# First block of a fused Fourier mixing and MLP kernel: the last product of each weight rounding on GpSimd, the other operations of the rounding reordered

## The chip, the cores and the metric

The kernel runs on one core of one Trainium2 chip. The metric is the device time in microseconds (us) of one execution; the median of three runs counts. The five engines of a core (TensorE, VectorE, ScalarE, GpSimd, SyncE; in the profile PE, DVE, ACT, POOL, SP) each work through an own queue in order and wait for each other by semaphores.

## The reference

```python
def reference(x, moe_w_in, moe_w_out):          # x: 8 x 3008 x 256, f32
    X = np.fft.fft(x, axis=1)
    X = np.fft.fft(X, axis=2)
    a = X.real.astype(np.float32).reshape(8 * 3008, 256)
    h = a @ moe_w_in                             # 256 x 2048
    g = np.maximum(h, 0.0) ** 2
    return (g @ moe_w_out).astype(np.float32)    # 2048 x 256
```

The two weight matrices arrive as 64-bit floats. The kernel reads each as pairs of 32-bit words (`low`, `high`) and rounds them to f32 on the chip.

## The kernel before, in words

The Fourier transform along the sequence is a set of matrix products with tables of cosines and sines. Symmetries are folded first, so that for each of the 8 sequences only 1505 columns remain; they lie in two tiles `Pt` and `Qt`, and a third, `Et`, holds one column spread over all partitions. The transform along the 256 features is merged into the first weight matrix: G1 and G2 are the products of the cosine and sine tables with `moe_w_in`.

After an opening (tables, the fold and transform of the first sequence, up to about 43 us) the kernel runs one long list of steps. A step is (sequence, block of 251 columns, j), with j from 0 to 7 (`NJ`), each j standing for two chunks of 128 of the 2048 hidden features. One step has these parts:

- `front`: for both chunks, TensorE multiplies `Pt` by G1 and `Qt` by G2 into a PSUM tile `ph` (L825, L826; two such tiles take turns). VectorE adds the `Et` part (L828, tile `he`) and forms sum and difference (L830, L831, tile `g`).
- `combine`: ScalarE takes relu and square of `g` (L840, L841). From step 8 on GpSimd also forms four sums `s` (L848 to L851) for a scheme with seven instead of eight products.
- `back`, two steps later (`LAG = 2`): TensorE multiplies `g` by `wout` into accumulators (L865 in the first block, with eight products a step; L878 with seven afterwards).

The first block (steps 0 to 7, sequence 0, columns 0 to 250) has more to do, since the weights are prepared there, just in time. For each j one tile `win` and one tile `wout` of 128 x 512 are loaded (`load`, SyncE, L259, into tiles `raw`) and rounded (`convert`). A rounding of one tile has, in the kernel before, eight operations on 128 x 512 elements: VectorE takes the exponent out of `high` (L274, tile `fd`); ScalarE turns it into a scale by two relus (L276, L277); VectorE takes the mantissa bits (L279, tile `m`); ScalarE scales `low` in place (L281); and then the function `finish` on VectorE puts the sign in (L284), adds `low` to the mantissa (L286) and multiplies mantissa and scale into the target (L287). Tiles `fd` come from a pool of two, tiles `m` from a pool of three.

`begin_win(j)` starts the rounding of `win` j; its second function `products` (TensorE L302, ScalarE L303) makes the chunks of G1 and G2, and its third, `for_e` (TensorE L311, VectorE L313), the factor `gE` that L828 uses. `load_wout(j)` starts the rounding of `wout` j.

The order within each engine's queue is the order of the Python calls; no scheduler changes it. In a step i of the first block `weights` calls, after `front`: the products of `win` i+1; the start of `wout` i-1; the end of `win` i+2 (`rounded`); the start of `win` i+3. The end of `wout` i-1 comes last in the step (`leftover`), ahead of L313 of `win` i+1. So VectorE has this order in a step: front, start of `wout`, end of `win`, start of the next `win`, end of `wout`, L313.

From step 10 on, VectorE and ScalarE fold the next sequence between the fronts (`ahead`, `between`).

Of the kernel before, what the change touches and what calls it, by code (L numbers as in the profile page):

```python
# [8 lines left out]
F32 = mybir.dt.float32  # L9
U32 = mybir.dt.uint32  # L10
AF = mybir.ActivationFunctionType
ALU = mybir.AluOpType
# [70 lines left out]
def kernel(  # L83
# [12 lines left out]
    nc = tc.nc  # L96
    B, NROW, _, D = x.shape
# [6 lines left out]
    NJ = NFC // 2  # L104
# [19 lines left out]
    op = ctx.enter_context(tc.tile_pool(name="op", bufs=2))  # L124
# [5 lines left out]
    tt = nc.vector.tensor_tensor  # L130
    act = nc.scalar.activation
# [81 lines left out]
    for i in range(2):  # L213
        nc.vector.tensor_scalar(out=signs[:, i:i + 1], in0=last, scalar1=(-2.0, 2.0)[i], scalar2=(1.0, -1.0)[i],
                                op0=ALU.mult, op1=ALU.add)
# [15 lines left out]
    def pair_in(j):  # L231

        return moe_w_in.rearrange("(c p) (h j f) -> j c p h f", p=P, j=NJ, h=2)[j]
# [5 lines left out]
    def parts(w, k):  # L239
        return w.rearrange("p c (e h) -> p h (c e)", h=k)  # L240
# [6 lines left out]
    def scratch():  # L247

        return sp.tile([P, 4 * CK], F32, name="m", tag="s")[:, 0:2 * CH].rearrange("p (c e) -> p c e", c=2)

    def load(src):

        nonlocal raws
        pool, tag = (gp, "g") if raws in (1, 2) else (xp, "x") if raws % (NX + 1) else (ep, "c")
        raws += 1
        single = src.dtype == F32
        raw = pool.tile([P, 2, CH, 1 if single else 2], src.dtype if single else U32, name="raw", tag=tag)
        for c in range(2):
            nc.sync.dma_start(out=raw[:, c].rearrange("p (o e) w -> p o (e w)", o=src.shape[2]),  # L259
                              in_=src[c] if single else src[c].bitcast(U32))  # L260
        return raw

    def convert(dst, raw):


        k = dst.shape[1]
        if raw.dtype == F32:
            return lambda: nc.vector.tensor_copy(dst, parts(raw[:, :, :, 0], k))
        low, high = raw[:, :, :, 0], raw[:, :, :, 1]
        m = scratch()  # L270
        e = fp.tile([P, 2, CH], F32, name="fd", tag="fd")
        mb, eb, rest = m.bitcast(U32), e.bitcast(U32), low.bitcast(F32)

        nc.vector.tensor_scalar(out=eb, in0=high, scalar1=20, scalar2=0x7FF,  # L274
                                op0=ALU.logical_shift_right, op1=ALU.bitwise_and)
        act(e, eb, AF.Relu, bias=ramp[:, 0:1], scale=-1.0)  # L276
        act(eb, e, AF.Relu, bias=ramp[:, 1:2], scale=-2.0 ** 23)  # L277

        nc.vector.tensor_scalar(out=mb, in0=high, scalar1=0xFFFFF, scalar2=0x100000,  # L279
                                op0=ALU.bitwise_and, op1=ALU.bitwise_or)  # L280
        act(rest, low, AF.Copy, scale=2.0 ** -32)  # L281

        def finish():
            nc.vector.scalar_tensor_tensor(out=eb, in0=high, scalar=0x80000000, in1=eb,  # L284
                                           op0=ALU.bitwise_and, op1=ALU.bitwise_or)
            tt(out=m, in0=mb, in1=rest, op=ALU.add)  # L286
            nc.vector.scalar_tensor_tensor(out=dst, in0=parts(m, k), scalar=2.0 ** -20, in1=parts(e, k),  # L287
                                           op0=ALU.mult, op1=ALU.mult)

        return finish  # L290


    def begin_win(j):

        w = ep.tile([P, 2, CH], F32, name="win", tag="sB" if j % 2 else "sA")
        finish = convert(parts(w, 1), win.pop(j, None) or load(pair_in(j)))

        def products():
            for tab, G, nm in ((cosd, G1, "mC"), (sind, G2, "mD")):
                pg = psm.tile([P, CH], F32, name="pg", tag=nm)  # L300
                for i in range(2):
                    nc.tensor.matmul(pg, tab[:, i], w[:, i], start=i == 0, stop=i == 1)  # L302
                nc.scalar.copy(G.rearrange("p (h j f) -> j p h f", h=2, j=NJ)[j],  # L303
                               pg.rearrange("p (h f) -> p h f", h=2))

        def for_e():

            ps = psd.tile([P, CH], F32, name="pe", tag="d")
            for h in range(2):
                fc = j + NJ * h  # L310
                nc.tensor.matmul(ps[:, h:h + 1], G2[:, fc * P:(fc + 1) * P], last, start=True, stop=True)  # L311

            return lambda: nc.vector.tensor_scalar_mul(gE[:, j::NJ], ps[:, 0:2], 0.5)  # L313

        win[j] = finish, products, for_e

    win = {}

    def load_wout(j):

        return convert(wout[:, j].rearrange("p h c e -> p h (c e)"), load(pair_out(j)))
# [477 lines left out]
    def spread_e():  # L799

        _, qt, et = PQE[0]
        ps = psd.tile([P, CH], F32, name="pe", tag="d")[:, 0:CK]
        nc.tensor.matmul(ps, last.to_broadcast([P, P]), qt[:, 0:CK], start=True, stop=True)
        nc.scalar.copy(et[:, 0:CK], ps)
# [10 lines left out]
    def front(b, k0, n, j, between):  # L815

        pt, qt, et = PQE[b]
        ks = slice(k0, k0 + n)
        g = gp.tile([P, 2, 2, CK], F32, name="g", tag="g")
        for h in range(2):  # L820
            fc = j + NJ * h
            fs = slice(fc * P, (fc + 1) * P)
            ps = psh.tile([P, 2, CH], F32, name="ph", tag="h")
            hP, hQ = ps[:, 0, 0:n], ps[:, 1, 0:n]
            nc.tensor.matmul(hP, G1[:, fs], pt[:, ks], start=True, stop=True)  # L825
            nc.tensor.matmul(hQ, G2[0:P - 1, fs], qt[0:P - 1, ks], start=True, stop=True)  # L826
            t = hp.tile([P, CK], F32, name="he", tag="he")[:, 0:n]
            nc.vector.scalar_tensor_tensor(out=t, in0=et[:, ks], scalar=gE[:, fc:fc + 1], in1=hP,  # L828
                                           op0=ALU.mult, op1=ALU.add)
            tt(out=g[:, h, 0, 0:n], in0=t, in1=hQ, op=ALU.add)  # L830
            tt(out=g[:, h, 1, 0:n][:, ::-1], in0=t, in1=hQ, op=ALU.subtract)  # L831
            between(h)
        return g
# [179 lines left out]
                groups[1, kp, nm]()  # L1013

    def rounded(j):
        win[j][0]()


    start()
# [50 lines left out]
    q_part("even0", "even1", "even2")  # L1070
    awake(12)
    rounded(1)
    for kp in range(2):
        for nm in ("join_4", "join_2", "lo"):
            groups[1, kp, nm]()
        if kp == 0:
            begin_win(2)
    spread_e()
    q_part("hi")
    copy_e()  # L1080
# [10 lines left out]
    def share(i):  # L1091
        return 0.0 if i < NJ + LAG + 2 else SHARE[i % NJ]
# [17 lines left out]
            f()  # L1110
            spent, room = spent + t, room - t

    late = []

    def weights():


        if i + 1 < NJ:
            win[i + 1][1]()
        now = i - 1 if i < NJ - 1 else i  # L1120
        if now >= 0:
            late.append(load_wout(now))
        if i + 2 < NJ:
            rounded(i + 2)
        if i + 3 < NJ:
            begin_win(i + 3)
        elif i == NJ - 2:
            late.append(load_wout(i))

    def leftover():  # L1130
        while late:
            late.pop(0)()

    flight, finished = [], []
    for i in range(len(steps) + LAG + 4):
        if i < len(steps):
            b, k0, n, j = steps[i]
            if i == NJ:
                for k in range(NX):
                    load_later(k)  # L1140
            if NJ <= i < NJ + NL:
                load_column(i - NJ)
            if i % per == 0:
                assert not side
                side = ahead(b + 1) if b + 1 < B else []
                spent, pace = 0.0, sum(t for t, _ in side) / sum(share(i + k) for k in range(per - 2))
            g = front(b, k0, n, j, between)
            if i < NJ:
                weights()
                s = combine(n, g, True)  # L1150
            elif i < 2 * NJ:
                leftover()
                if j < 4:
                    sum_wout(slice(j // 2 * (NJ // 2), (j // 2 + 1) * (NJ // 2)), j % 2)
        while finished and finished[0][0] <= i:
            store(*finished.pop(0)[1:])
        if i >= LAG and flight:
            at, g_, s_ = flight.pop(0)
            final = at[:3] == (B - 1, *BLOCKS[-1])
            back(at[2], at[3], g_, s_, final)  # L1160
            if at[3] == NJ - 1:
                c_ = gather(at[2], s_ is None, final)
                finished += [(i + 2 + s, *at[:3], s, c_, final) for s in range(2)]
        if i + 1 < NJ:
            late.append(win[i + 1][2]())
            leftover()
        if i < len(steps):
            flight.append(((b, k0, n, j), g, s if i < NJ else combine(n, g, False)))
# [63 lines left out]
```

## Time and profile before

| | before |
|---|---|
| median of 3 runs | 1924.22 us (1923.99 to 1924.96) |
| the profiled execution | 1924.01 us, of which span 1922.2 us |
| TensorE busy | 1909.9 us, 99% of the span |
| VectorE busy | 1451.7 us, 76% |
| ScalarE busy | 957.3 us, 50% |
| GpSimd busy | 1110.5 us, 58% |
| mean granted TensorE clock | 0.999 |
| L287, 128 x 512, first block | 16 times, 0.69 to 0.70 us each |
| L284 and L286 | 16 times each, 0.69 us each |
| L274 and L279 | 16 times each, 0.42 us each |

The span runs from the first to the last instruction; the execution's time has 1.8 us around it. The busy time of an instruction is longer than its place in the queue where the next one may start before it ends: four L274 or L279 in a row start 0.335 us apart, two independent operations of 0.69 us start 0.60 us apart. A wait in the profile names the instruction that waited, the one that released it, and the time that its engine stood idle.

### The profile page before, as it was taken

How to read it: one execution, taken by the hardware profiler on the slowest of the kernel's cores; microseconds unless marked ns; L12 is line 12 of the kernel's file. 1: busy time of each engine (PE TensorE's matmuls, PEld its weight loads, DVE VectorE, ACT ScalarE, POOL GpSimd, SP SyncE). 2: the span in 40 equal slices, each digit the busy share in tenths (PEclk: the TensorE clock that was granted, in tenths of full speed). 3: DMA queues.
4: the chain of work that ended last, by engine and by line, in shares of the span. 5: the costliest groups of instructions: out<-in, count | busy, mean ns of one | idle time of the engine just before them, and what ended most of it. 6: DMA issues, size and time to landing. Idle time of an engine off the chain costs nothing.

```text
span 1922.2 us, 28182 instructions
## 1 busy us (share of the span) xinstructions
PE 1909.9 (99%) x9270; PEld 1700.5 (88%) x9270; DVE 1451.7 (76%) x3654; ACT 957.3 (50%) x1209; POOL 1110.5 (58%) x1701
## 2 busy tenths in 40 slices
PE   9999999999999999999999999999999999999998
PEld 7888898888988898888988889888898888988887
DVE  8998887887677876788668887788767877655554
ACT  2855554455454554545445454455544555444444
POOL 0055665666566655665665666566656666566565
PEclk9999999999999999999999999999999999999999
DMA  8331111110111101111011110111001101100100
GB/s 216 117 38 37 44 40 31 34 41 17 28 36 35 40 12 36 28 47 28 12 36 39 39 26 12 45 37 36 21 20 46 36 12 22 27 12 12 22 11 23
DMA packets 146622, 69.58 MB, mean 36 GB/s; under 512 B 130145, under 2 KB 137259, under 8 KB 146474
## 3 DMA queue, kind: packets, MB, share of 16 engines
q1 hardware_dynamic: 146022, 66.87, 14.0%
q8 instruction: 73, 1.20, 0.3%
q14 instruction: 75, 0.61, 0.1%
q0 software_dynamic: 176, 0.65, 0.1%
q10 hardware_dynamic: 276, 0.26, 0.0%
HBM read 43.03 MB, written 24.69 MB: 35 GB/s over the span
## 4 chain that ended last, share of the span: by engine, by line
PE 94%; DVE 3%; DMA 1%; issue 0%; ACT 0%; SPq 0%; DVEq 0%; ACTq 0%
PE ph L825 16%; PE ph L826 16%; PE mC L878 16%; PE mA L878 16%; PE mB L878 16%; PE mD L878 8%; PE pd L727 1%; PE pd L619 1%; PE pd L701 1%; DMA xt<-in_x_dram 1%; DMA cosT<-in_cos_s_dram 0%; DVE he L828 0%; DVE m L286 0%; DVE g L831 0%; DMA sind<-in_sin_d_dram 0%
## 5 line engine op out<-in xcount | busy, mean ns | idle before, releaser
L840 ACT ACTIVATE g<-g 128x1004 f32<-128x1004 f32 (+1 forms) x384 | 399.0, 1039 | 689.4 <-DVE g L831 425.2
L848 POOL TENSOR_TENSOR s<-g 128x251 f32<-128x251 f32 (+1 forms) x376 | 237.2, 631 | 689.8 <-ACT g L841 628.3
L828 DVE SCALAR_TENSOR_TENSOR he<-Et,gE,ph 128x251 f32<-128x251 f32 (+1 forms) x768 | 362.4, 472 | 340.4 <-PE ph L826 336.0
L825 PE MATMUL ph<-Pt,G 128*128 128x251 f32 (+1 forms) x1536 | 453.2, 376 | 0.0
L826 PE MATMUL ph<-Qt,G 127*128 127x251 f32 (+1 forms) x1536 | 452.2, 375 | 0.0
L841 ACT ACTIVATE g<-g 128x1004 f32<-128x1004 f32 (+1 forms) x384 | 399.3, 1040 | 12.2
L878 PE MATMUL mC<-s,wsum 128*128 128x251 f32 (+1 forms) x1504 | 381.4, 374 | 0.0
L878 PE MATMUL mA<-g,wout 128*128 128x251 f32 (+1 forms) x1504 | 380.1, 374 | 0.0
L830 DVE TENSOR_TENSOR g<-he,ph 128x251 f32<-128x251 f32 (+1 forms) x768 | 320.3, 417 | 53.5 <-DVE he L828 1.8
L826 PEld LDWEIGHTS ph<-Qt,G 127*128 127x128 f32 x1536 | 291.9, 190 | 35.9
L825 PEld LDWEIGHTS ph<-Pt,G 128*128 128x128 f32 x1536 | 285.8, 189 | 34.3 <-DVE g L831 0.4
L878 PEld LDWEIGHTS mC<-s,wsum 128*128 128x128 f32 x1504 | 285.5, 190 | 34.5
L831 DVE TENSOR_TENSOR g<-he,ph 128x251 f32<-128x251 f32 (+1 forms) x768 | 314.0, 409 | 0.0
L878 PEld LDWEIGHTS mA<-g,wout 128*128 128x128 f32 x1504 | 282.6, 189 | 35.3 <-issue 0.3
L849 POOL TENSOR_TENSOR s<-s,g 128x251 f32<-128x251 f32 (+1 forms) x376 | 271.5, 722 | 29.5
L850 POOL TENSOR_TENSOR s<-g 128x251 f32<-128x251 f32 (+1 forms) x376 | 273.2, 726 | 0.0
L851 POOL TENSOR_TENSOR s<-g,s 128x251 f32<-128x251 f32 (+1 forms) x376 | 241.6, 643 | 0.0
L878 PE MATMUL mB<-g,wsum 128*128 128x251 f32 (+1 forms) x752 | 220.5, 374 | 0.0
L878 PE MATMUL mD<-s,wout 128*128 128x251 f32 (+1 forms) x752 | 220.3, 374 | 0.0
L878 PE MATMUL mB<-s,wout 128*128 128x251 f32 (+1 forms) x752 | 219.9, 374 | 0.0
L878 PEld LDWEIGHTS mB<-g,wsum 128*128 128x128 f32 x752 | 142.6, 190 | 17.4
L878 PEld LDWEIGHTS mD<-s,wout 128*128 128x128 f32 x752 | 141.9, 189 | 17.7
(174 smaller groups left out, 1389.0 us busy)
## 6 DMA issues: line engine op xcount, KB each, us to landing
out_dram<-os SPq DMA_DIRECT2D x376, 56.0 KB
xt<-in_x_dram SPq DMA_DIRECT2D x39, 384.0 KB
xt<-in_x_dram SPq DMA_DIRECT2D x63, 128.0 KB
Et<-e_dram SPq DMA_DIRECT2D x7, 752.5 KB
out_dram<-os SPq DMA_DIRECT2D x288, 6.8 KB
raw<-in_moe_w_in_dram SPq DMA_DIRECT2D x16, 256.0 KB
raw<-in_moe_w_out_dram SPq DMA_DIRECT2D x16, 256.0 KB
xt<-in_x_dram SPq DMA_DIRECT2D x2, 512.0 KB
```

The costliest lines, as they stand in the source:

```text
L825: nc.tensor.matmul(hP, G1[:, fs], pt[:, ks], start=True, stop=True)
L826: nc.tensor.matmul(hQ, G2[0:P - 1, fs], qt[0:P - 1, ks], start=True, stop=True)
L828: nc.vector.scalar_tensor_tensor(out=t, in0=et[:, ks], scalar=gE[:, fc:fc + 1], in1=hP, op0=ALU.mult, op1=ALU.add)
L830: tt(out=g[:, h, 0, 0:n], in0=t, in1=hQ, op=ALU.add)
L831: tt(out=g[:, h, 1, 0:n][:, ::-1], in0=t, in1=hQ, op=ALU.subtract)
L840: act(v, v, AF.Relu)
L841: act(v, v, AF.Square)
L848: gt(out=s1, in0=g21, in1=g22, op=ALU.add)
L849: gt(out=s2, in0=s1, in1=g11, op=ALU.subtract)
L850: gt(out=s3, in0=g11, in1=g21, op=ALU.subtract)
L851: gt(out=s4, in0=g12, in1=s2, op=ALU.subtract)
L878: nc.tensor.matmul(acc[nm][:, i, 0:n], w, v[:, 0:n], start=j == 0 and i == 0, stop=j == NJ - 1, skip_group_check=True)
```

## The change

The rounding changes in three ways. First, its arithmetic: ScalarE now scales the mantissa in place (L281: `m` by 2^-20) instead of `low`; the addition becomes one operation that scales `low` by 2^-52 and adds `m`; the last product becomes a plain product of two tiles, which any engine with a product can do. `convert` returns two functions, `halves` (sign and addition, VectorE) and `product(engine)`.

Second, the engine: in the first block the product is done by GpSimd; the two roundings of the opening (`win` 0 and 1) keep it on VectorE.

Third, the order. What was started in step i-1 is ended at the beginning of step i, ahead of its front (`rounding`): the `halves` of the tile started last come first, the products come in the order of the starts. After the front, `weights` calls the products of `win` i+1, the start of `win` i+3 and the start of `wout` i (step 5 starts `wout` 5 and 6, step 6 `wout` 7). So VectorE has this order in a step: `halves` of `wout` i-1, `halves` of `win` i+2, front, start of `win` i+3, start of `wout` i, L313. In the changed kernel the line numbers behind the rounding are one higher (L825 becomes L826, L311 becomes L312).

```diff
@@ convert
-        mb, eb, rest = m.bitcast(U32), e.bitcast(U32), low.bitcast(F32)
+        mb, eb = m.bitcast(U32), e.bitcast(U32)
...
-        act(rest, low, AF.Copy, scale=2.0 ** -32)
-
-        def finish():
+        act(m, mb, AF.Copy, scale=2.0 ** -20)
+
+        def halves():
             nc.vector.scalar_tensor_tensor(out=eb, in0=high, scalar=0x80000000, in1=eb,
                                            op0=ALU.bitwise_and, op1=ALU.bitwise_or)
-            tt(out=m, in0=mb, in1=rest, op=ALU.add)
-            nc.vector.scalar_tensor_tensor(out=dst, in0=parts(m, k), scalar=2.0 ** -20, in1=parts(e, k),
-                                           op0=ALU.mult, op1=ALU.mult)
-
-        return finish
+            nc.vector.scalar_tensor_tensor(out=m, in0=low, scalar=2.0 ** -52, in1=m, op0=ALU.mult, op1=ALU.add)
+
+        def product(engine):
+            engine.tensor_tensor(out=dst, in0=parts(m, k), in1=parts(e, k), op=ALU.mult)
+
+        return halves, product
@@ rounded (opening)
-        win[j][0]()
+        halves, product = win[j][0]
+        halves()
+        product(nc.vector)
@@ the steps
-    late = []
+    late, open_ = [], [begun]          # begun: win 2, started in the opening
+
+    def rounding():
+
+        for halves, _ in reversed(open_):
+            halves()
+        while open_:
+            open_.pop(0)[1](nc.gpsimd)
 
     def weights():
         if i + 1 < NJ:
             win[i + 1][1]()
-        now = i - 1 if i < NJ - 1 else i
-        if now >= 0:
-            late.append(load_wout(now))
-        if i + 2 < NJ:
-            rounded(i + 2)
         if i + 3 < NJ:
             begin_win(i + 3)
-        elif i == NJ - 2:
-            late.append(load_wout(i))
+            open_.append(win[i + 3][0])
+        for k in (i, i + 1)[i > NJ - 3:1 + (NJ - 3 <= i < NJ - 1)]:
+            open_.append(load_wout(k))
...
+            if i < NJ:
+                rounding()
             g = front(b, k0, n, j, between)
             if i < NJ:
                 weights()
                 s = combine(n, g, True)
             elif i < 2 * NJ:
-                leftover()
```

## Prediction before the run

> **What bounds the kernel now.** I read the page first: its chain that ended last gives the split of the whole span.
>
> ```profile
> PE 94%; DVE 3%; DMA 1%; issue 0%; ACT 0%; SPq 0%; DVEq 0%; ACTq 0%
> ```
>
> TensorE carries nearly everything. The change touches only the first block (steps 0 to 7, about 43 to 98 us). So the second view is busy time by stretch, cut to that block: PE, PEld, DVE, ACT, POOL, then the granted clock.
>
> ```profile
> 46.70:53.00 6.30, 4.14 (x20) 3.40 (x20) 6.09 (x16) 4.42 (x9) 0.00 (x0) 1.00 0.28 102
> 53.00:57.00 4.00, 3.85 (x13) 3.25 (x14) 3.78 (x9) 3.93 (x8) 0.00 (x0) 0.61 0.42 131
> 64.40:71.60 7.20, 7.20 (x37) 6.46 (x36) 6.95 (x17) 5.81 (x10) 0.00 (x0) 1.00 0.34 113
> 71.60:78.90 7.30, 7.30 (x38) 6.51 (x38) 7.01 (x17) 5.94 (x10) 0.00 (x0) 1.00 0.40 136
> 86.20:94.00 7.80, 7.47 (x37) 6.33 (x36) 7.01 (x17) 5.23 (x10) 0.00 (x0) 1.00 0.18 67
> ```
>
> TensorE is full from 57 to 86 us and has holes only before and after. The third view, the waits, prices them.
>
> ```profile
> PE pe L311 <- ACT G L303: 2.7, 2, 2.3
> PE mA L865 <- DVE wout L287: 0.6, 1, 0.6
> ```
>
> So TensorE loses 3.3 us to waits. The granted clock fell after the 2.3 us hole: (1 - 0.61) x 4.00 = 1.56 us lost there, and 0.15 more in the next stretch (0.98 over 7.4 us), 1.7 in all. 5.0 us is therefore about all that a faster VectorE could win here. The fourth view is VectorE's queue over one step, in order of time.
>
> ```profile
> 72.79 0.48 DVE L828 SCALAR_TENSOR_TENSOR he<-Et,gE,ph 128x251 f32<-128x251 f32 x1
> ...
> 75.12 0.42 DVE L274 TENSOR_SCALAR fd<-raw 128x512 uint32<-128x512 uint32 x1
> ...
> 76.40 0.69 DVE L286 TENSOR_TENSOR m<-m,raw 128x512 f32<-128x512 uint32 x1
> 77.12 0.69 DVE L287 SCALAR_TENSOR_TENSOR win<-m,fd 128x512 f32<-128x512 f32 x1
> ...
> 79.84 0.69 DVE L287 SCALAR_TENSOR_TENSOR wout<-m,fd 128x512 f32<-128x512 f32 x1
> 80.72 0.47 DVE L828 SCALAR_TENSOR_TENSOR he<-Et,gE,ph 128x251 f32<-128x251 f32 x1
> ```
>
> One step of VectorE is 80.72 - 72.79 = 7.93 us with no idle gap; TensorE needs 7.27 us (L302's first start goes 64.36, 71.63, 78.90). VectorE drifts later by 0.66 us a step while TensorE works off its lead. What matters of the old order: between a rounding's first operations (L274, L279) and its last ones VectorE always has another weight tile's operations, so ScalarE's three operations in between are hidden.
>
> **What the change removes.** Per step the two products (L287) leave VectorE: each spans 0.72 us from start to next start, 1.4 us in all. The remaining work of a step is front 75.12 - 72.79 = 2.33, four starts at 0.335, four `halves` operations at 0.60, one L313 at 0.2: 6.3 us, below TensorE's 7.27. L286 becomes another two-input operation of the same shape (0.68 against 0.69 for the neighbouring forms), and ScalarE's L281 now reads and writes `m` at the same 512 elements: an operation of the same size on the same engine replaces each, so both cost nothing. The same holds for the two roundings of the opening, whose product stays on VectorE.
>
> **What it moves.** In the new order VectorE's queue in a step is: front(i), L274 and L279 of `win` i+3, L274 and L279 of `wout` i, L313, then the `halves` of that `wout`, then of that `win`, then front(i+1). Between the starts and the first `halves` only L313 is left. The `halves` of `wout` need ScalarE's six operations (three for `win`, then three for `wout`), and in VectorE's queue the next front is behind them. That is a walk from VectorE to ScalarE and back inside each step. The loads move no queue: SyncE still issues `win` 3, `wout` 0, `win` 4, `wout` 1 and so on, each when a raw tile comes free, which now happens after the `halves`, a step ahead of the use; before, the last ones were issued by 85.4 us. The last `wout` roundings leave step 8 for steps 6 and 7, so the x tiles of the next sequence, which reuse those buffers and are first read in step 10, do not come later relative to the steps. ScalarE does two roundings back to back in one place of the trace:
>
> ```profile
> 52.99 0.73 ACT L276 ACTIVATE fd<-fd,ramp 128x512 f32<-128x512 uint32 x1
> ...
> 56.32 0.66 ACT L281 ACTIVATE raw<-raw 128x512 f32<-128x512 uint32 x1
> ```
>
> That is 56.32 + 0.66 - 52.99 = 3.99 us. The walk, from one L274 to the next step's L274: L274 to ScalarE's L276 0.46 (75.12 to 75.58), six operations 3.99, signal 0.04, then L286 of `wout`, L284 and L286 of `win` 3 x 0.60 = 1.80, front 2.33: **8.62 us a step** against 7.93 before and TensorE's 7.27. Behind the waiting `halves` stand the front's L828, so the ph buffers come free late and TensorE waits for them.
>
> From the start: L313 at 43.07, two `halves` of `win` 2 (ScalarE finished it at 42.02) to 44.42, so front 0 starts at 44.42 (43.81 before), and L274 of `win` 3 at 46.75. Front 1 is 4.49 + 1.80 = 6.29 later, at 53.04 (48.99 before). Front 6 is 5 x 8.62 later, 96.14 (87.89 before). Step 6 rounds one tile only: front 2.33, then 0.46 + 0.76 + 0.62 + 0.68 + 0.04 = 2.56, L286 0.60, front 7 at 101.63. TensorE's front 8 needs the first ph buffer of front 7, 0.85 + 0.41 + 0.04 = 1.30 later: 102.93, where before it started at 97.76. With 0.14 more between the halves of that front (a wait of 0.32 against 0.18 before) the sum is **+5.3 us**. From there TensorE is full in both, so nothing is won back. The 3.3 us of waits and the 1.7 us of slow clock are inside the old 97.76 and are not added again; a slow stretch early in the block would be hidden, as TensorE waits 1.3 us a step anyway.
>
> **What it adds.** Two products a step on GpSimd. No row has that shape. Nearest:
>
> ```profile
> L850 POOL TENSOR_TENSOR s<-g 128x251 f32<-128x251 f32 (+1 forms) x376 | 273.2, 726 | 0.0
> 46.08 0.57 POOL L809 DMA_DIRECT2D Et<-e_dram  x1 [1.94 <-DMA e_dram<-Qt]
> ```
>
> 251 elements take 0.63 (L848) to 0.72. Scaled by 2.04 that is 1.47 at most; with 0.10 fixed, as the smallest memset (103 ns), 0.63 gives 0.53 x 2.04 + 0.10 = 1.18. GpSimd is otherwise empty in this block, after the two `e_dram` transfers it issues until 46.65. `win` i+2 is needed a step later and `wout` i two fronts later, so the product's length alone is hidden behind the walk. It is not hidden from VectorE:
>
> ```profile
> 153.56 0.64 POOL L851 TENSOR_TENSOR s<-g,s 128x251 f32<-128x251 f32 x1
> 153.80 0.67 DVE L492 TENSOR_TENSOR sc<-fd 95x254 f32<-95x254 f32 x1
> ```
>
> L492 is 0.41 where GpSimd rests and 0.67 here: it ran only when L851 was over at 154.20. Operations with a PSUM input beside GpSimd (L828, L830, L831) keep 0.47, 0.42, 0.41. So the fronts run free beside the products, but the L274 behind them may be held. L274 has one input, and the trace never shows it beside GpSimd; the bounds are no hold, and a hold to the end of the second product. The first product starts when L286 of `win` is done, 5.69 + 0.69 + 0.04 = 6.42 into the walk; the second ends 2P later. With P = 1.18 the next L274 comes at 6.42 + 2.36 + 0.04 = 8.82 (+0.20 a step), with 1.47 at 9.40 (+0.78). There are six such steps, and in step 0 the product begins at 46.65, which delays L274 of `win` 3 by P - 0.06. Hold: 1.12 + 6 x 0.20 = +2.3 up to 1.41 + 6 x 0.78 = +6.1. I take the hold (the nearest row, and L274 works on SBUF alone at 0.42 for 512 elements) with P = 1.18 (the slope of the shorter row): 5.3 + 2.3 = **+7.6**.
>
> Against that stands a rule of the Trainium skill, which speaks against this change: the page SBUF — State Buffer, section "SBUF: two separate sides", says that GpSimd and a VectorE operation in a two-port mode or with two SBUF inputs exclude each other for a whole instruction. By it L274 is held as well; without it the sum would be +5.3. The GPSIMD Engine Reference, section "Elementwise — side-by-side cycle accounting", measures two-input operations on GpSimd at 1.96 times VectorE; by it P would be about 0.69 x 1.96 = 1.35, an estimate, and the sum +9.8.
>
> **Rivals.** *The holes close* (faster): if ScalarE's second rounding overlapped the `halves`, so that the walk fell below 7.27, TensorE would be full from step 1 and 2.3 + 0.6 + 1.7 = 4.6 us would go: 1919.4. For it: VectorE's sum is only 6.3. Against it: `halves` of `wout` wait for the last of the six ScalarE operations. It decides once 1.35 us are missing from the walk; one rounding of ScalarE is 2.0. *A draw*: a walk of 7.9 to 8.1, within 2 us of before. *GpSimd becomes the bound* (slower still): at P = 2.0, for example if the two-element stride of the `wout` product costs it dearly, the walk is 6.42 + 4.0 + 0.04 = 10.46: 5.3 + 1.94 + 6 x 1.84 = +18.3, 1942.3. It begins to decide at P = 1.08.
>
> **How the numbers follow.** The profiled execution took 1924.01 us (span 1922.2), 0.2 below the median 1924.22. 1924.0 + 7.6 = 1931.6. Chances: walk with or without hold 0.80, GpSimd bound 0.06, draw 0.07, holes close 0.07. The measurement tells 0.2% (3.8 us) from no change, so +5.3 and above counts as slower: 0.86; draw 0.07; faster 0.07. Range: from a walk 0.3 us a step shorter without hold (+3.5, 1927.5) to P = 1.47 with hold plus 0.6 (1936.0); outside it are the holes closing, GpSimd as bound and half of the draw, 0.17.
>
> **What would show it.** Right: in the first block VectorE idles about 2 us a step before L284 or L286, released by ScalarE's L281; fronts come 8.6 to 9.4 us apart; TensorE waits at L826 and L312 in every step and its front 8 starts near 105. The hold: L274 longer than 0.42, ending after a GpSimd product. Wrong: TensorE full from 54 us on, or fronts at most 7.9 us apart, or idle VectorE released by GpSimd rather than ScalarE.

## The result, and the profile after

The changed kernel takes 1933.55 us (median of 5 runs, 1933.01 to 1934.56) against 1924.22 us: +9.3 us, ratio 1.0048 (95% interval 1.0033 to 1.0062). The forecast was 1931.6 with a range of 1927.5 to 1936.0. The profiled execution took 1933.17 us, span 1931.4, against 1924.01 and 1922.2 before.

The chain that ended last hardly differs over the whole span; ScalarE enters it with 1%:

```profile
PE 93%; DVE 3%; ACT 1%; DMA 1%; issue 0%; SPq 0%; DVEq 0%; ACTq 0%
```

Busy time by stretch in the first block (PE, PEld, DVE, ACT, POOL, clock) says more:

```profile
53.00:57.00 4.00, 2.38 (x10) 1.78 (x11) 3.93 (x9) 1.49 (x3) 2.72 (x2) 0.90 0.37 118
65.28:74.39 9.11, 8.01 (x37) 6.43 (x36) 6.69 (x16) 6.33 (x10) 2.73 (x3) 1.00 0.25 80
93.00:102.00 9.00, 7.86 (x37) 6.33 (x37) 6.58 (x16) 6.32 (x10) 2.71 (x3) 1.00 0.27 90
```

TensorE was full from 57 to 86 us before; now it has about a microsecond of idle time in every step. VectorE, packed before, works 6.7 of 9.1 us. No engine is busy all the time: the signature of a chain that goes round between engines. The waits of the block name it:

```profile
DVE fd L284 <- ACT fd L277: 14.2, 7, 2.4
...
PE pe L312 <- ACT G L304: 7.8, 6, 3.1
PEld ph L826 <- DVE g L832: 3.4, 7, 0.9
```

VectorE's L284 waits for ScalarE's L277 in each of seven steps, 2.35 us in most of them. In TensorE's queue the late copies of G (L304) and the late front (L832, which frees `ph`) are the echo. One step of VectorE in order of time:

```profile
65.28 0.94 DVE L274 TENSOR_SCALAR fd<-raw 128x512 uint32<-128x512 uint32 x1
...
67.15 0.15 DVE L314 TENSOR_SCALAR gE<-pe 128x2 f32<-128x2 f32 x1
69.66 0.69 DVE L284 SCALAR_TENSOR_TENSOR fd<-raw,fd 128x512 uint32<-128x512 uint32 x1 [2.35 <-ACT fd L277]
...
72.08 0.46 DVE L829 SCALAR_TENSOR_TENSOR he<-Et,gE,ph 128x251 f32<-128x251 f32 x1
...
74.39 0.96 DVE L274 TENSOR_SCALAR fd<-raw 128x512 uint32<-128x512 uint32 x1
```

From L274 to L274 it is 9.11 us. Five of ScalarE's six operations lie between the L274 and the L284, which starts when the second L277 is done (68.90 + 0.72 = 69.62):

```profile
66.26 0.72 ACT L276 ACTIVATE fd<-fd,ramp 128x512 f32<-128x512 uint32 x1 [2.70 <-DVE fd L274]
...
68.90 0.72 ACT L277 ACTIVATE fd<-fd,ramp 128x512 uint32<-128x512 f32 x1
69.53 0.61 ACT L281 ACTIVATE m<-m 128x512 f32<-128x512 uint32 x1
```

And L274, 0.42 us long elsewhere, takes 0.94 while GpSimd is still at work (the short product below tests that this is the cause):

```profile
63.21 1.27 POOL L289 TENSOR_TENSOR win<-m,fd 128x512 f32<-128x512 f32 x1 [6.38 <-DVE m L286]
64.44 1.50 POOL L289 TENSOR_TENSOR wout<-m,fd 128x512 f32<-128x512 f32 x1
```

The second product ends at 65.94, the L274 at 66.22. Where the time is lost can be read from one number: TensorE's front 8 starts 55.06 us after its front 0 before (42.70 to 97.76) and 63.63 us after it now (43.24 to 106.87), +8.57. From front 8 to front 12 it is 19.85 and 19.97 us: nothing is won back. The remaining 0.54 us lie in the opening. Over the twelve kernels of this study front 0 starts anywhere from 42.01 to 44.04 us, although ahead of it only the arithmetic of three roundings differs, and in one kernel a memset. So the length of the block is the better measure of these kernels, and is given for each below; it comes from one profiled execution of each kernel.

### The profile page after: what moved, and what is told of

It reads as the page before. It is cut to its first block, busy times and chain, and to the rows that moved or that the text cites. A ratio compares the mean times of both kernels' runs of the same rounds, so it can differ in the third digit from the quotient of the medians.

```text
span 1931.4 us, 28176 instructions
## 1 busy us (share of the span) xinstructions
PE 1913.1 (99%) x9270; PEld 1700.0 (88%) x9270; DVE 1443.9 (75%) x3640; ACT 956.3 (50%) x1209; POOL 1127.4 (58%) x1715
## 4 chain that ended last, share of the span: by engine, by line
PE 93%; DVE 3%; ACT 1%; DMA 1%; issue 0%; SPq 0%; DVEq 0%; ACTq 0%
PE ph L826 16%; PE mC L879 16%; PE mA L879 16%; PE ph L827 16%; PE mB L879 16%; PE mD L879 8%; PE pd L728 1%; PE pd L620 1%; DMA xt<-in_x_dram 1%; PE pd L702 1%; DMA cosT<-in_cos_s_dram 0%; DVE m L286 0%; DVE he L829 0%; ACT fd L277 0%; DVE g L832 0%; ACT fd L276 0%
## 5 line engine op out<-in xcount | busy, mean ns | idle before, releaser
L829 DVE SCALAR_TENSOR_TENSOR he<-Et,gE,ph 128x251 f32<-128x251 f32 (+1 forms) x768 | 362.4, 472 | 344.6 <-PE ph L827 340.7
L826 PE MATMUL ph<-Pt,G 128*128 128x251 f32 (+1 forms) x1536 | 453.9, 376 | 0.9 <-DVE g L832 0.5
L826 PEld LDWEIGHTS ph<-Pt,G 128*128 128x128 f32 x1536 | 285.2, 189 | 37.8 <-DVE g L832 3.8
L832 DVE TENSOR_TENSOR g<-he,ph 128x251 f32<-128x251 f32 (+1 forms) x768 | 314.1, 409 | 0.0
```

## The experiments

The theory: the new order makes a walk VectorE, ScalarE, VectorE in every step, 8.6 us long, and the product of `wout` on GpSimd holds the next L274 for another half microsecond. The main rival: GpSimd's part in the block is what costs, and the order is harmless. All interval statements are against the kernel before, run beside.

| kernel | median, us | ratio (95%) | front 0 to front 8, us |
|---|---|---|---|
| before | 1924.2 to 1924.5 | | 55.06 |
| changed | 1933.55 | 1.0048 (1.0033 to 1.0062) | 63.63 |
| new order, products on VectorE | 1939.30 | 1.0080 (1.0065 to 1.0095) | 70.11 |
| new order, short product of wout | 1930.39 | 1.0029 (1.0018 to 1.0041) | 61.17 |
| new order, tiles in order of start | 1927.10 | 1.0014 (1.0005 to 1.0023) | 57.86 |
| same, win's product on VectorE | 1925.31 | 1.0003 (0.9994 to 1.0013) | 56.57 |
| same, and later relu | 1924.20 | 0.9997 (0.9988 to 1.0007) | 53.72 |
| old order, both products on GpSimd | 1925.29 | 1.0005 (0.9996 to 1.0014) | 56.07 |
| old order, new arithmetic alone | 1924.85 | 1.0003 (0.9993 to 1.0012) | 55.00 |
| old order, wout's product on GpSimd | 1923.01 | 0.9992 (0.9983 to 1.0001) | 53.09 |
| same, later relu in step 0 | 1922.28 | 0.9987 (0.9978 to 0.9996) | 53.09 |
| same, first wout on VectorE | 1922.19 | 0.9989 (0.9980 to 0.9998) | 53.75 |

**New order, products back on VectorE.**

```diff
-            open_.pop(0)[1](nc.gpsimd)
+            open_.pop(0)[1](nc.vector)
```

> The changed order, but both products of a step are done by VectorE again. Theory (the order makes a walk VectorE, ScalarE, VectorE inside each step, 9.11 us long with the hold): the hold of L274 (0.52) goes, two products of 0.6 to 0.7 us come onto the walk, so 9.11 - 0.52 + 1.3 = 9.9 us a step, and the time is 1937 to 1940. Rival (GpSimd is what costs: its products are long and hold VectorE): the loss goes, 1923 to 1926.

1939.3 us, as the theory had it. VectorE's fronts (L829) come 9.93 us apart (65.09, 75.02), the wait for ScalarE is still 2.35 us, and the two products lie on the walk:

```profile
71.27 0.69 DVE L284 SCALAR_TENSOR_TENSOR fd<-raw,fd 128x512 uint32<-128x512 uint32 x1 [2.35 <-ACT fd L277]
...
73.80 0.69 DVE L289 TENSOR_TENSOR win<-m,fd 128x512 f32<-128x512 f32 x1
74.41 0.69 DVE L289 TENSOR_TENSOR wout<-m,fd 128x512 f32<-128x512 f32 x1
```

So GpSimd is a help inside the new order, worth 5.7 us (6.5 in the block), and the main rival falls.

**The old order with both products on GpSimd.** The kernel before with the new `convert`; in the steps, `rounded(i + 2)` and the end of `wout` use GpSimd.

```diff
-            rounded(i + 2)
+            rounded(i + 2, nc.gpsimd)
...
-            late.append(load_wout(now))
+            late.append(later_end(load_wout(now)))     # halves, then product(nc.gpsimd)
```

> The order of the kernel before with the new arithmetic, and in the steps of the first block the products on GpSimd. Theory (the order is what costs): no walk; VectorE's 7.93 us a step lose two products of 0.72, and the L274 of the next win, which comes straight behind the halves of win, waits about 1.4 us for GpSimd's product of win: 7.7 us a step, 1922 to 1924.5. Rival (GpSimd's part is what costs): most of the loss stays, 1929 to 1933.

1925.29 us, 0.8 above the expected band: the loss of 9 us is gone, but nothing is won. Fronts are 7.94 us apart (65.84, 73.78), where 7.7 was expected: VectorE gives up two products of about 0.7 us each and waits as long for GpSimd's product of `win`, since the next `win` needs the `fd` tile that the product still reads.

```profile
70.30 1.29 POOL L289 TENSOR_TENSOR win<-m,fd 128x512 f32<-128x512 f32 x1 [3.06 <-DVE m L286]
71.62 0.43 DVE L274 TENSOR_SCALAR fd<-raw 128x512 uint32<-128x512 uint32 x1 [1.50 <-POOL win L289]
```

Here the delay is a wait (idle time 1.50 ahead of a short L274). In the changed kernel it is a hold: no idle time, and an L274 of twice the length. Holds occur here too, but only at the ends of the block (an L279 of 1.50 us in step 0, an L286 of 1.76 and an L284 of 1.55 in the last steps); the block is 1.0 us longer than before.

**The old order with the new arithmetic alone**, all products on VectorE (the same kernel with `nc.vector` in both places).

> The kernel before with the new arithmetic alone: old order, all products on VectorE, ScalarE scales m instead of low. Theory (the arithmetic costs nothing): within 1 us of before, 1923.5 to 1925.5. Rival (part of the loss is in the new forms): more than 2 us slower.

1924.85 us and a block of 55.00 us against 55.06: the arithmetic costs nothing that could be measured. With this run the four combinations of order and engine are complete: in the old order the block takes 55.00 us (products on VectorE) or 56.07 (on GpSimd), in the new order 70.11 or 63.63.

**The hold alone.** The product of `wout` on GpSimd covers 16 of 256 columns of each half; the rest of `wout` stays zero.

```diff
+            n = 16 if k == 2 else 2 * CH
-            engine.tensor_tensor(out=dst, in0=parts(m, k), in1=parts(e, k), op=ALU.mult)
+            engine.tensor_tensor(out=dst[:, :, 0:n], in0=parts(m, k)[:, :, 0:n], in1=parts(e, k)[:, :, 0:n], op=ALU.mult)
```

> As the changed kernel, but GpSimd's product of wout covers only 16 of 256 columns of each half (the rest of wout is left at zero, from a memset that GpSimd does in the opening), so that it takes about 0.2 us instead of 1.50 and is over before L274 comes. Theory: L274 is 0.42 instead of 0.94 long, the walk 8.59 instead of 9.11, six steps: -3.1 to -3.4, 1930 to 1930.5. Rival 1 (no hold, the stretched L274 costs nothing): 1933.5. Rival 2 (all of the loss is the hold): 1924 to 1926.

1930.39 us, -3.2 against the changed kernel, inside the expected band; both rivals fall. The product takes 0.26 us, and L274 is short again while the wait for ScalarE is unchanged:

```profile
65.43 0.42 DVE L274 TENSOR_SCALAR fd<-raw 128x512 uint32<-128x512 uint32 x1
...
69.28 0.69 DVE L284 SCALAR_TENSOR_TENSOR fd<-raw,fd 128x512 uint32<-128x512 uint32 x1 [2.35 <-ACT fd L277]
```

The next L274 comes at 74.03: a bare walk of 8.60 us. The block says a little less than the median: it is 2.46 us shorter, not 3.2. From front 1 to front 7 3.2 us are won (48.48 us against 51.69), but step 0 takes 0.77 longer, since its L274 starts at 47.08, meets the product of `win` from 47.10 on, and takes 1.59 us with ScalarE's work waiting behind it. That the median came out inside the band is in part luck.

**The tiles in the order of their starts.**

```diff
-        for halves, _ in reversed(open_):
+        for halves, _ in open_:
```

> As the changed kernel, but the halves are taken in the order of the starts: win first, then wout. Theory: ScalarE has finished win's three operations 1.9 us before wout's, so win's halves (1.2 us) fall into the wait. Two outcomes: if the product of win on GpSimd holds L284 of wout (two inputs in SBUF), the walk is 8.1 us a step and the time about 1927; if it doesn't, 7.4 us and 1922 to 1923. Rival (the length of the GpSimd work sets the step): no change, 1932 to 1934.

1927.10 us: one word is worth 6.5 us (5.8 in the block). The fronts come 8.10 us apart (69.56, 77.66), the first of the two cases. `win` was ready on ScalarE first, so its halves fill the wait; but then GpSimd's product of `win` runs while VectorE wants the halves of `wout`, and L284 takes 1.40 instead of 0.69:

```profile
75.31 1.27 POOL L289 TENSOR_TENSOR win<-m,fd 128x512 f32<-128x512 f32 x1 [4.08 <-DVE m L286]
75.73 1.40 DVE L284 SCALAR_TENSOR_TENSOR fd<-raw,fd 128x512 uint32<-128x512 uint32 x1 [0.59 <-ACT fd L277]
```

**The same, with the product of `win` on VectorE**, where it falls into the wait.

```diff
-        for halves, _ in reversed(open_):
+        while open_:
+            halves, product = open_.pop(0)
             halves()
-        while open_:
-            open_.pop(0)[1](nc.gpsimd)
+            product(nc.gpsimd if not open_ else nc.vector)
```

> The changed kernel with the tiles rounded in the order of their starts, the product of win on VectorE (it falls into the wait for ScalarE) and only the product of wout on GpSimd. Theory: no GpSimd product runs beside an operation of VectorE that reads SBUF alone, so the hold is gone and the walk is 0.46 + 3.4 + 2 x 0.6 + 2.33 = 7.4 us; VectorE then runs about even with TensorE's 7.27 and the time is near before, 1923 to 1925. If another hold appears, the walk is above 8 and the time above 1927.

1925.31 us, 0.3 above the band. The fronts are 7.4 us apart (75.84, 83.27, 90.69), as worked out, but for 7.95 us once in step 2, where VectorE waits 1.0 us for TensorE. No L274 or L284 is held but one: in step 0 the product of `win` 2 is still on GpSimd, and L274 takes 1.68 us beside it. The block is still 1.5 us longer than before: TensorE waits 4.0 us (50.89 to 54.84) for the copies of G in step 1, and its clock is at half from 53.01 to 59.84 us.

**The same, and relu and square behind the next copies of G.**

```diff
             win[i + 1][1]()
+        while held:
+            combine(*held.pop(0), True)     # of step i - 1
...
-                s = combine(n, g, True)
+                s = held.append((n, g)) if i < NJ - 1 else combine(n, g, True)
```

> The same, and ScalarE takes relu and square of a step's g after the next step's copies of G (not ahead of them), so that TensorE's wait of 2 to 3 us for these copies in step 1 gets shorter. Theory: that wait falls to about 1 us and the slow clock behind it goes: 1 to 3 us less than without it, 1921 to 1923.5. Rival (the wait is hidden behind VectorE anyway): no change against the split alone.

1924.20 us, above the band, but the block is 53.72 us, 2.9 shorter than without: the longest wait for L304 falls from 4.0 to 1.4 us and there is no slow stretch. The medians differ by 1.1 us with a spread of over 2 us each, so the block carries this reading, not the median. How much of the 2.9 us is the shorter wait and how much the clock was not separated.

**The old order, and only the product of `wout` on GpSimd**, in three forms: as it is; with relu and square of step 0 behind the next copies; and with the first `wout` on VectorE besides.

```diff
     def later_end(parts_):
-        return lambda: end(parts_, nc.vector)
+        return lambda: end(parts_, nc.gpsimd)
```

> Old order with wout's products on GpSimd, and nothing else: relu and square of step 0 stay ahead of the copies of G. Theory: VectorE's relief (0.6 us a step) removes TensorE's late waits for wout and the late front 7, but the wait of 2.3 us in step 1 and the slow clock behind it stay: half of the gain, 1922.5 to 1924. Rival (all of the gain is VectorE's relief): 1921 to 1922.5, as with the later relu.

> Old order and new arithmetic, product of win on VectorE, product of wout on GpSimd, where only L313 and the front follow on VectorE (no hold); and in step 0 alone ScalarE's relu and square come after the next copies of G. Theory: 7.93 - 0.6 = 7.3 us a step on VectorE without a wait, as long as TensorE's step, and TensorE's wait in step 1 falls from 2.3 to below 1 us: front 8 some 3 us earlier, 1920 to 1922.5. Rival (anything on GpSimd in this block costs): above 1924.

> As old order with wout's products on GpSimd, but the first wout's product is left on VectorE, since TensorE waited 1.5 us for it in step 2 (0.69 instead of 1.5 us long). Theory: 0.5 to 1 us less than without, 1920.5 to 1922. Rival (VectorE's 0.6 us more in step 1 come back as a later front 2): no change, 1922 to 1923.

The plain form takes 1923.01 us (interval 0.9983 to 1.0001), inside the band of its theory, with a block of 53.09 us; the later relu gives 1922.28, inside its band, and the same 53.09, though it cuts the longest wait for L304 from 2.2 to 0.5 us. So the wait itself is hidden, as the rival had it, and the 2.0 us of the block are VectorE's relief. The slow clock behind the wait is another matter. The profiled execution of the plain form had none; its mean clock was 1.000, as in two others, and these three took 1920.6 to 1921.4 us. Two others had 0.999 (1923.1 and 1923.3 us) and six 0.998 (1922.3 to 1924.7). All ten executions with the later relu had 0.999 or 1.000 (1920.9 to 1925.0). This fits the theory that the slow clock takes back part of the gain, but no trace shows one of the executions with a lower clock.

L289 of `wout` is gone from VectorE's queue. L314 and the front follow on L286 without a hold, although GpSimd's product runs beside them; they have an input in PSUM:

```profile
69.41 0.71 DVE L286 SCALAR_TENSOR_TENSOR m<-raw,m 128x512 f32<-128x512 uint32 x1
70.01 0.18 DVE L314 TENSOR_SCALAR gE<-pe 128x2 f32<-128x2 f32 x1
70.30 0.48 DVE L829 SCALAR_TENSOR_TENSOR he<-Et,gE,ph 128x251 f32<-128x251 f32 x1
...
70.20 1.51 POOL L289 TENSOR_TENSOR wout<-m,fd 128x512 f32<-128x512 f32 x1 [5.71 <-DVE gE L314]
```

One hold is left in all three forms: near the end of the block, where two roundings of `wout` follow each other, an L284 takes 1.54 us.

The first `wout` on VectorE gains nothing (1922.19 us, as the rival had it; the block is 0.7 us longer). The forms with the later relu beat the kernel before by about 2 us, with intervals that end just below 1, and the changed kernel by 11.

## Why the prediction was right, and where it was off

- **The mechanism** stood: VectorE idles before L284, released by ScalarE, and TensorE waits at the copies and (mostly in its weight loads) at `ph` in each step. The walk without a hold was put at 8.62 us; the short product shows 8.60. One detail was off: L284 waits for the second L277, not L281, and ScalarE's six operations take 69.53 + 0.61 - 66.26 = 3.88 us instead of 3.99. The walk therefore has five of ScalarE's operations and four of the `halves` (69.66 to 72.08, 2.42 us) instead of six and three (1.80). The two nearly cancel, and that the sum came out so closely is luck.
- **The mis-sized term is the hold.** P was taken as 1.18 us for both products; they measured 1.27 (`win`) and 1.50 (`wout`), the latter just above the upper bound of 1.47. A held step is 9.11 us instead of 8.82: 5 x 0.29 = +1.45. In step 6 two products of `wout` run, L274 takes 1.08 and front 7 comes 6.16 us behind front 6 instead of 5.69: +0.47.
- **The hold in step 0 was wrong in its place.** L274 of `win` 3 was to be held for 1.12 us; it started at 47.20, before GpSimd's first product at 47.82 (the second `e_dram` transfer was issued at 47.24 instead of 46.08), and took 0.42. The L279 behind it was held instead:

```profile
47.54 1.86 DVE L279 TENSOR_SCALAR m<-raw 128x512 uint32<-128x512 uint32 x1
...
47.82 1.28 POOL L289 TENSOR_TENSOR win<-m,fd 128x512 f32<-128x512 f32 x1
```

- **The sum.** The start of `wout` 0 came only at 49.33, but VectorE then waited 1.32 us for ScalarE instead of 2.35. Front 1 comes 9.00 us behind front 0 instead of 9.74: -0.74. The three differences add up to +1.18; from VectorE's front 0 to TensorE's front 8 it is 61.99 us against a forecast of 60.83. Another 0.46 lies ahead: VectorE's front 0 started at 44.88 instead of 44.42. Together that is nearly all of the 1.7 us between +7.6 and +9.3.
- **The two rules weighed.** The Trainium skill, page SBUF — State Buffer, section "SBUF: two separate sides", speaks of exclusion for the whole instruction; L274 at 0.94 beside the product and 0.42 without it agree, as does L284 at 1.40. L284 has two inputs in SBUF, which the forecast's reading of the rule names; L274 has one, and no trace shows its mode, so the hold rests on the measurement. From the skill's GPSIMD Engine Reference, section "Elementwise — side-by-side cycle accounting", P was estimated at 1.35, between the two measured values, and the sum at +9.8; measured is +9.3. It is this near partly by luck: that sum has 1.29 us of hold in step 0, where 0.4 was lost.
- **The rivals.** The holes did not close; a draw is what the old order with GpSimd gives; GpSimd did not become the bound.
- **Wrong on the side:** the forecast put 5.0 us as about the most that a faster VectorE could win, 1.7 of it slow clock. The old order with the new arithmetic ran without a slow stretch, and its block is 55.00 us against 55.06: that loss was hidden. What a lighter VectorE did win in the block is 55.06 - 53.09 = 2.0 us. The slow stretch of the changed kernel (56.20 to 59.61 us) was hidden, as forecast: the fronts are 9.07 us apart across it and 9.10 to 9.13 afterwards. And L287 of `wout` spans 0.61 us to the next start (79.84 to 80.45), not 0.72; VectorE's sum was not the limit, so nothing follows from it.

## What to carry to other kernels

Moving work off a full engine is worth nothing if the new order puts another engine's answer between two of its operations: walk once round the dependent chain, engine by engine, and compare its length with the busiest engine's sum. Where one engine can hold another, ask not only how long the moved operation is but what runs beside it: here a product was free next to operations with an input in PSUM, and it doubled the length of those that work on SBUF alone. The smallest version, one product moved and VectorE's order kept, is 2.0 us shorter in the block; its median is lower by 1.2 us, not quite clear of the noise, and by 2.1 with relu and square of step 0 moved as well.

## What the runs showed of the hardware

- Two GpSimd products of 128 x 512 differ: about 1.27 us for `win` (read in a row; 1.27 to 1.29 in the changed kernel) and 1.50 for `wout`, whose inputs are read at a stride of two elements. That the stride is the cause was not tried.
- A one-input VectorE operation on SBUF (L274: 0.42 us alone, 0.94 beside a product) is held by GpSimd like a two-input one (L284: 0.69 and 1.40); the trace shows a hold as a longer operation without idle time ahead of it.
- TensorE's clock changed on a fixed grid. Stretches at half clock in the first block lasted 3.41 or 6.83 us, and the full clock ahead of the first one lasted 47.79 us in six kernels and 51.20 in the changed one, which is 14 and 15 times 3.41. The Trainium skill, page TensorE: Matmul & The Clock Gate, section "What's actually happening", has free-running windows of that length; these traces agree.
- What counted was the idle time inside one such window, not the length of a wait. With the time cut on this grid, counted from the start of the first full-clock stretch, of the windows in the block that ran at full clock, those in which TensorE was idle for 1.79 us or more were all followed by half clock, and those with 1.41 us or less never; in between, 1.49 (old order, both products on GpSimd) and one of two windows with 1.53 were. The same wait of 2.2 to 2.3 us in step 1 fell into one window in the kernel before (2.26 us, then half clock) and was cut in two in the old order with the new arithmetic (1.09 and 1.12) and in the plain form with `wout` on GpSimd (1.41 and 0.80), which kept the full clock.
